# Softmaxes as separate steps, and every compute queue held to the order of the text, in a kernel of a Fourier transform and a soft mixture of experts

## The chip, the cores and the metric

The kernel runs on one core of a Trainium2 chip. The metric is the device time of one execution in microseconds. A core has five engines that run their own queues of instructions in order: TensorE (PE in the profile, with its weight loads as PEld), VectorE (DVE), ScalarE (ACT), GpSimd (POOL), and SyncE (SP), which here issues all transfers (DMA). Matmuls write to PSUM, in eight banks; VectorE and ScalarE copy results from there to SBUF ("evict" them), from where transfers take them to memory.

## The reference

The input x has 8 sequences of 2496 rows of 256 numbers, in fp32. A two-dimensional Fourier transform is taken of each sequence and its real part goes through a mixture of experts in which every token reaches every slot:

```python
X = np.fft.fft(np.fft.fft(x, axis=1), axis=2).real      # then 19968 tokens of 256
logits = tokens @ phi                                   # 32 slots
d = softmax of logits over the tokens
slot_input = d.T @ tokens                               # 8 experts, 4 slots each
h = np.maximum(slot_input[e] @ w1[e], 0.0)              # 256 -> 1024
slot_out[e] = h @ w2[e]                                 # 1024 -> 256
c = softmax of logits over the slots                    # per token
out = c @ slot_out
```

The sums in both softmaxes get 1e-9 added before the division. The output, 19968 rows of 256, is 20.4 MB.

## The kernel before, in words

The sequences are worked in four pairs, p = 0 to 3. Each pair goes through parts named by letters: a (loads are folded and projected on the slots), t, b and c (the transform's steps on the projected data, which end in the logits lt[p], their exponentials and maxima), e, d and u (the transform back, and the sum of tokens for each slot). The part m joins the four pairs' sums, l does the experts' first layer (hidden tiles h, hs, hT), v the second (so), and r spreads the experts' result over the partitions as rh, the experts' sum.

What follows concerns the output's weights c. Part s of a pair turns its logits by TensorE transposes (three PSUM banks cT, copied by ScalarE to a tile c of 128 partitions, 40 rows and 32 slots), and does the softmax over the slots in two pieces of 16 and 24 rows: VectorE takes the maximum (L531), GpSimd subtracts it (L532), ScalarE takes the exponential (L533), VectorE sums, adds 1e-9 and takes the reciprocal (L534 to L536), GpSimd multiplies (L537). Part q transposes a piece on VectorE into ct (L542). Part o makes one block of output, (p, b) with b = 0 to 4: four matmul tiles po, one for each row group g of 32 partitions of TensorE (tile_position (32 g, 0), L562), each in a PSUM bank of its own taken in turn from seven, copied by ScalarE and VectorE alternately into an output tile o (L566), and one transfer of the whole block (L570; block (0,0) goes in four). In blocks 0 to 3 a tile is one matmul of 512 columns, in block 4 two of 256 or 192. In the profile every fp32 matmul counts as two instructions. The output tiles share a ring of six with the loads of x and w1.

The text calls the parts in the order of the table ORDER. It is not the order of the queues: a scheduler takes the instructions of all parts, with the text's order as their priority, and places them engine by engine by its own estimate of when each is ready. Only SP's output transfers stand in the text's order, block after block. The parts s and q are held behind the last matmul of u by `after`. What is issued by the parts up to v keeps this freedom in both kernels.

Of the kernel before, what the change touches and what calls it, by code (L numbers as in the profile page):

```python
# [6 lines left out]
F32 = mybir.dt.float32  # L7
F32R = mybir.dt.float32r
AF = mybir.ActivationFunctionType
ALU = mybir.AluOpType  # L10
AX = mybir.AxisListType
# [3 lines left out]
NA, NCF, NKC = 64, 39, 20  # L15
NPAIR = 4
D = 256
NSLOT = 32
GS = 3
NG = 11  # L20
# [3 lines left out]
CAFTER = 1  # L24
# [4 lines left out]
CT = ['sa', 'lt', 'lt', 'lt']  # L29
HT = ['se', 'zs']  # L30
KP = ((0, 16), (16, 24))
# [14 lines left out]
).split()  # L46


# [68 lines left out]
def _build(nc, tc, xh, phih, w1h, w2h, cins, where, out):  # L117
    from contextlib import ExitStack, nullcontext

    v, sc, pe = nc.vector, nc.scalar, nc.tensor  # L120
    ctx = ExitStack()
    with ctx:
        cp = ctx.enter_context(tc.tile_pool(name="cp", bufs=1))
        sb = ctx.enter_context(tc.tile_pool(name="sb", bufs=1))
# [16 lines left out]
        def bufs_(tag):  # L141
            return {"zs": 2, "sa": 2, "se": SEB, "lt": LT}[tag]

        def bank(name, dt=F32):
            return pp.tile([128, 512], dt, name=name, tag="ps")
# [4 lines left out]
        def bank1(name, dt=F32):  # L150
            return p1.tile([128, 512], dt, name=name, tag="p1")
# [25 lines left out]
        def C(name):  # L177
            i, o, r, w = where[name]
            return cs[i][:r, o : o + w]

        ident = C("ident")
# [3 lines left out]
        ps = bank("psphi")  # L185
# [234 lines left out]
        anchor = {}  # L420
# [44 lines left out]
        def part_l(eh):  # L465
            for fh in range(2):
                ps = bank(f"h{eh}{fh}")
                for lc in range(2):
                    for g in range(4):
                        ins = pe.matmul(  # L470
                            ps[32 * g : 32 * g + 32, :], sT[:, lc, :], w1t[eh, fh, lc, g],
                            start=lc == 0, stop=lc == 1, tile_position=(0, 32 * g),
                        )
                        anchor.setdefault("l", ins.ins)
                hs = sb.tile([128, 512], F32, name=f"hs{eh}{fh}", tag="dpm", bufs=2)
                mask = sm[:, 16 + eh : 17 + eh]
                if HA:
                    sc.activation(hs, ps, AF.Relu, scale=mask)
                else:
                    v.tensor_scalar(hs, ps, 0.0, mask, op0=ALU.max, op1=ALU.mult)  # L480
                hT[eh, fh] = et([128, 16, NSLOT], f"hT{eh}{fh}")
                v.transpose(hT[eh, fh].rearrange("p f s -> p (f s)"), hs)

        def part_v(eh):
            if eh == 0:
                sos_.append(pu.tile([128, 512], F32, name="so", tag="u"))
            so = sos_[0]
            for f in range(8):
                for g in range(4):
                    ins = pe.matmul(  # L490
                        so[32 * g : 32 * g + 32, 0:D], hT[eh, f // 4][:, 4 * (f % 4) + g, :],
                        w2t[eh, f][:, g, :],
                        start=eh == 0 and f == 0, stop=eh == 1 and f == 7, tile_position=(0, 32 * g),
                    )

            anchor[f"v{eh}"] = ins.ins

        def part_r():
            so = sos_[0]
            rh.append(sb.tile([128, D], F32, name="rh", tag="mex2", bufs=1))  # L500
            sos = sb.tile([128, D], F32, name="sos", tag="dpm", bufs=2)
            ps = bank("sorep")
            sc.copy(sos[:, :128], so[:, :128])
            v.tensor_copy(sos[:, 128:], so[:, 128:D])
            for k in range(2):
                dk = slice(128 * k, 128 * k + 128)
                pe.matmul(ps[:, dk], C("sel2"), sos[:, dk], start=True, stop=True)
            v.tensor_copy(rh[0], ps[:, :D])

        hl, cq = {}, {}  # L510

        def part_s(p):
            L = lt[p]
            cq[p] = sb.tile([128, 40, NSLOT], F32, name=f"c{p}", tag=CT[p], bufs=bufs_(CT[p]))
            for b in range(3):
                ps = bank1(f"cT{p}_{b}")
                n = min(4, NG - 4 * b)
                for j in range(n):
                    pe.transpose(  # L519
                        ps[:, 120 * j : 120 * j + 120],  # L520
                        L[:, 4 * b + j].rearrange("p s k -> p (s k)"), ident[:120, :120],
                    )
                w = min(GS * n, NSLOT - 12 * b)
                sc.copy(  # L524
                    cq[p][:, :, 12 * b : 12 * b + w].rearrange("p (k h) s -> p k h s", h=2),
                    ps[:, : 40 * w].rearrange("p (s h k) -> p k h s", h=2, k=NKC),
                )
            for i, (r0, n) in enumerate(KP):
                c = cq[p][:, r0 : r0 + n]
                m = sb.tile([128, 2, 24], F32, name=f"cm{p}_{i}", tag="cm", bufs=2)[:, :, :n]  # L530
                v.tensor_reduce(m[:, 0], c, axis=AX.X, op=ALU.max)  # L531
                nc.gpsimd.tensor_tensor(c, c, m[:, 0].unsqueeze(2).to_broadcast([128, n, NSLOT]), op=ALU.subtract)  # L532
                sc.activation(c, c, AF.Exp)  # L533
                v.tensor_reduce(m[:, 1], c, axis=AX.X, op=ALU.add)  # L534
                v.tensor_scalar(m[:, 1], m[:, 1], 1e-9, None, op0=ALU.add)
                v.reciprocal(m[:, 1], m[:, 1])  # L536
                nc.gpsimd.tensor_tensor(c, c, m[:, 1].unsqueeze(2).to_broadcast([128, n, NSLOT]), op=ALU.mult)  # L537

        def part_q(p, i):
            r0, n = KP[i]  # L540
# [30 lines left out]
                    done = o  # L571

        def after(f, *a):
            at_ = {0: None, 1: anchor.get("u"), 2: anchor.get("l")}[CAFTER]
            if at_ is None:
                return f(*a)
            with tc.issue_after(at_):
                return f(*a)

        parts = {  # L580
            "a": part_a, "t": lambda p, _: part_t(p), "b": lambda p, _: part_b(p), "c": part_c,
            "e": part_e, "d": part_d, "u": lambda p, _: part_u(p), "w": lambda *_: load_w(),
            "m": lambda *_: part_m(), "l": lambda i, _: part_l(i), "v": lambda i, _: part_v(i),
            "r": lambda *_: part_r(), "s": lambda p, _: after(part_s, p), "q": lambda p, i: after(part_q, p, i), "o": part_o,
        }
        for what in ORDER:
            parts[what[0]](int(what[1]), int(what[2]))


# [54 lines left out]
```

## Time and profile before

| | |
|---|---|
| median of 3 runs | 203.22 us (203.19 to 204.41) |
| profiled execution | 203.3 us |
| its span | 201.5 us |
| mean granted TensorE clock | 0.896 |
| TensorE, VectorE, ScalarE, GpSimd busy | 172.6, 129.0, 110.7, 20.8 us |
| transfers | 59.16 MB, of which 20.45 MB written |

Times in the profile are microseconds from the span's start unless marked ns. A group's row gives line, engine, operation, output and input tiles (without their numbers), shape and count, then the busy time, the mean ns of one, the idle time of the engine just before them and what ended it. A row of a stretch gives, for PE, PEld, DVE, ACT and POOL, the busy time and in brackets the number of instructions that began there; then the granted clock (1.00 is full), the mean busy share of the 16 DMA engines and GB/s. A piece of the chain of waits gives start, duration and what ran; the chain is followed back from the last instruction. A busy PE is modelled, and is not PE at its peak.

### The profile page before, as it was taken

The numbers are of one execution on the slowest core, as the hardware profiler recorded it, in microseconds if no ns is written. First come the engines' busy times: TensorE is split into PE (matmuls) and PEld (weight loads), VectorE is DVE, ScalarE is ACT, GpSimd is POOL, SyncE is SP. The second block draws the span as 40 slices with busy tenths as digits, with TensorE's granted clock in tenths as the row PEclk, the third lists the DMA queues.
The fourth block names the chain that finished last, engine by engine and source line by source line (L and its number), as shares of the span: only waits on it lengthen the run. The fifth ranks groups of instructions, "written<-read, shape, count | busy, mean of one in ns | idle before, by whom it ended". The sixth has DMA issues, their size and how long they took to land.

```text
span 201.5 us, 4131 instructions
## 1 busy us (share of the span) xinstructions
PE 172.6 (86%) x1644; PEld 114.0 (57%) x1644; DVE 129.0 (64%) x236; ACT 110.7 (55%) x247; POOL 20.8 (10%) x25
## 2 busy tenths in 40 slices
PE   0499999899999999899999899998996999989200
PEld 0475676476678786568658593455554465756100
DVE  0599859999959936522577247977878714868300
ACT  2125775679665967677569737414947205627200
POOL 0000000000000000000000007451015204400000
PEclk9999999999999999999999999999996555557955
DMA  5999999999941998003925879911994995849994
GB/s 180 410 429 411 418 414 428 415 420 369 342 192 34 358 411 339 6 0 95 314 115 181 338 220 367 411 60 54 408 412 170 415 416 211 351 197 416 423 419 175
DMA packets 10530, 59.16 MB, mean 294 GB/s; under 512 B 1296, under 2 KB 1680, under 8 KB 5520
## 3 DMA queue, kind: packets, MB, share of 16 engines
q1 hardware_dynamic: 10512, 58.91, 74.1%
q8 instruction: 13, 0.21, 0.4%
q14 instruction: 5, 0.04, 0.1%
HBM read 38.46 MB, written 20.45 MB: 292 GB/s over the span
## 4 chain that ended last, share of the span: by engine, by line
PE 73%; ACT 7%; DVE 6%; issue 3%; DMA 2%; POOL 1%; POOLq 1%; DVEq 0%; SPq 0%; ACTq 0%
PE po L562 15%; PE pt L231 9%; PE z L238 8%; PE e L329 6%; PE a L273 5%; PE u L371 5%; PE d L346 4%; PE h L470 4%; PE so L490 3%; PE cT L519 3%; PE lp L291 3%; PE lm L292 3%; DMA x<-xh 2%; DVE o L566 2%; ACT et L232 2%
## 5 line engine op out<-in xcount | busy, mean ns | idle before, releaser
L562 PE MATMUL po<-ct,rh 32*128 32x512 f32 (+2 forms) x192 | 43.8, 700 | 2.9 <-DVE o L566 2.4
L562 PEld LDWEIGHTS po<-ct,rh 32*128 32x128 f32 x192 | 25.6, 239 | 17.7 <-DVE o L566 7.5
L231 PE MATMUL pt<-cs,eo 128*128 128x128 f32 x160 | 26.3, 295 | 8.9 <-DVE eo L226 7.8
L232 ACT COPY et<-pt 128x512 f32<-128x512 f32 x40 | 23.1, 594 | 13.8 <-PE pt L231 13.3
L566 ACT COPY o<-po 128x512 f32<-128x512 f32 (+1 forms) x40 | 21.3, 580 | 15.8 <-PE po L562 15.7
L566 DVE COPY o<-po 128x512 f32<-128x512 f32 (+1 forms) x40 | 24.6, 662 | 7.2 <-PE po L562 7.2
L231 PEld LDWEIGHTS pt<-cs,eo 128*128 128x128 f32 x160 | 19.3, 149 | 15.9 <-DVE eo L226 7.8
L224 DVE TENSOR_TENSOR x<-x 128x1024 f32<-128x1024 f32 x16 | 19.4, 1213 | 2.8 <-DMA x<-xh 2.8
L238 PE MATMUL z<-et,wphi 128*32 128x256 f32 (+1 forms) x288 | 19.0, 371 | 0.8 <-ACT et L232 0.8
L532 POOL TENSOR_TENSOR c<-c,cm 128x512 f32<-128x512 f32 (+1 forms) x8 | 10.0, 1264 | 75.3 <-DVE cm L531 72.2
L314 ACT ACTIVATE d<-lt,nm 120x128 f32<-120x128 f32 x44 | 13.6, 392 | 2.1 <-DVE nm L311 2.0
L226 DVE TENSOR_TENSOR eo<-x 128x512 f32<-128x512 f32 x20 | 13.6, 681 | 0.6 <-PE u L371 0.3
L227 DVE TENSOR_TENSOR eo<-x 128x512 f32<-128x512 f32 x20 | 13.6, 678 | 0.0
L329 PE MATMUL e<-cs,dpm 120*64 120x120 f32 x176 | 13.5, 273 | 0.0
L329 PEld LDWEIGHTS e<-cs,dpm 120*64 120x64 f32 x176 | 10.7, 136 | 3.5 <-issue 2.0
L238 PEld LDWEIGHTS z<-et,wphi 128*32 128x32 f32 x288 | 7.8, 113 | 8.3 <-ACT et L232 3.2
L354 ACT COPY ds<-d 64x320 f32<-64x320 f32 x24 | 10.0, 420 | 4.1 <-PE d L346 3.4
L273 PE MATMUL a<-cs,zt 128*120 128x128 f32 x88 | 11.4, 280 | 0.6 <-ACT zt L264 0.6
L371 PE MATMUL u<-eo,ds 128*32 128x129 f32 x320 | 11.6, 275 | 0.0
L524 ACT COPY c<-cT 128x480 f32<-128x480 f32 (+1 forms) x12 | 6.0, 516 | 10.3 <-PE cT L519 10.3
L273 PEld LDWEIGHTS a<-cs,zt 128*120 128x120 f32 x88 | 10.2, 183 | 1.9 <-ACT zt L264 1.3
L537 POOL TENSOR_TENSOR c<-c,cm 128x512 f32<-128x512 f32 (+1 forms) x8 | 10.1, 1263 | 8.4 <-DVE cm L536 8.4
(91 smaller groups left out, 213.5 us busy)
## 6 DMA issues: line engine op xcount, KB each, us to landing
x<-xh SPq DMA_DIRECT2D x16, 1024.0 KB, 11.4
out<-o SPq DMA_DIRECT2D x15, 1024.0 KB, 6.6
w<-w1h SPq DMA_DIRECT2D x6, 1024.0 KB, 9.0
w<-w2h SPq DMA_DIRECT2D x12, 512.0 KB, 6.3
x<-xh SPq DMA_DIRECT2D x4, 896.0 KB, 10.6
out<-o SPq DMA_DIRECT2D x4, 896.0 KB, 9.2
w<-w1h SPq DMA_DIRECT2D x4, 512.0 KB, 5.7
w<-w2h SPq DMA_DIRECT2D x2, 1024.0 KB, 8.3
```

The source lines that it names most:

```text
L224: v.tensor_tensor(x[:, 0:4], x[:, 0:4], x[:, 4:8], op=ALU.add)
L226: v.tensor_tensor(e[:, :, 0:128], x[:, 0:4, 0:128], x[:, 0:4, 128:256], op=ALU.add)
L227: v.tensor_tensor(e[:, :, 128:256], x[:, 0:4, 0:128], x[:, 0:4, 128:256], op=ALU.subtract)
L231: pe.transpose(b[:, g * 128 : g * 128 + 128], e[:, g, k * 128 : k * 128 + 128], ident)
L232: sc.copy(tr[k][:, :, :, qi, :], b.rearrange("p (g h a) -> p g h a", g=4, h=2))
L238: pe.matmul(z[32 * g : 32 * g + 32, o : o + n], wphi[:, w, :], tr[k][:, g].rearrange("p h q a -> p (h q a)"), start=i != 1, stop=i != 0, t ...
L273: pe.matmul(ps[:120, i * 128 : i * 128 + 128], zt[p][:, GS * g : GS * g + GS].rearrange("p s h c -> p (s h c)"), C("wa"), start=True, stop ...
L314: sc.activation(d[:, g], L[:, g], AF.Exp, bias=nm[:, g : g + 1], scale=1.0)
L329: pe.matmul(ps[64 * k : 64 * k + 64, 120 * i : 120 * i + 120], dpm[p, hf][:, k, 3 * j + i, :], C(name), start=True, stop=True, tile_positi ...
L371: last = pe.matmul(ub[32 * g : 32 * g + 32, 0:129], dsb[p][:, k, c, :], e[:, 0:129] if k == 0 else e[:, 127:256], start=cc == 0, stop=cc == 9,
L562: pe.matmul(po[:, j * w : j * w + w], rh[0][rows, 128 * dc : 128 * dc + 128], mv, start=True, stop=True, tile_position=(32 * g, 0),)
L566: (v.tensor_copy if n_ev[0] % 2 else sc.copy)(ot[:, o : o + w * len(dcs)], po[:, : w * len(dcs)])
```

## The change

The table ORDER is rewritten from the experts on. Part s becomes four steps: s (one of three groups of transposes and its copy), x (maximum and subtraction of one piece), y (its exponential), z (sum, reciprocal and multiplication). They are called one by one: the softmaxes of pairs 0 and 1 among the experts' layers, those of pairs 2 and 3 between the blocks of output of the pairs before. The parts' arithmetic is the same.

From part r on, each instruction of TensorE, VectorE, ScalarE and GpSimd gets an edge to the one that the text issued before it on the same engine. The edge orders the queue when the program is built and adds no wait on the chip. The output's transfers on SP stand as before.

```diff
@@ -40,9 +40,9 @@
...
-    "u30 m00 l00 s00 l10 q00 s10 v00 q01 v10 r00 o00 o01 q10 o02 q11 o03 "
...
+    "o00 s20 o01 s21 q11 o02 s22 o03 x20 x21 o04 y20 o10 y21 z20 o11 z21 s30 o12 q20 s31 o13 s32 x30 o14 q21 x31 "
...
@@ -509,32 +509,44 @@
 
         hl, cq = {}, {}
 
-        def part_s(p):
+        cm = {}
+
+        def part_s(p, b):
             L = lt[p]
-            cq[p] = sb.tile([128, 40, NSLOT], F32, name=f"c{p}", tag=CT[p], bufs=bufs_(CT[p]))
-            for b in range(3):
-                ps = bank1(f"cT{p}_{b}")
-                n = min(4, NG - 4 * b)
-                for j in range(n):
-                    pe.transpose(
-                        ps[:, 120 * j : 120 * j + 120],
-                        L[:, 4 * b + j].rearrange("p s k -> p (s k)"), ident[:120, :120],
-                    )
-                w = min(GS * n, NSLOT - 12 * b)
-                sc.copy(
-                    cq[p][:, :, 12 * b : 12 * b + w].rearrange("p (k h) s -> p k h s", h=2),
-                    ps[:, : 40 * w].rearrange("p (s h k) -> p k h s", h=2, k=NKC),
+            if b == 0:
+                cq[p] = sb.tile([128, 40, NSLOT], F32, name=f"c{p}", tag=CT[p], bufs=bufs_(CT[p]))
+            ps = bank1(f"cT{p}_{b}")
+            n = min(4, NG - 4 * b)
+            for j in range(n):
+                pe.transpose(
+                    ps[:, 120 * j : 120 * j + 120],
+                    L[:, 4 * b + j].rearrange("p s k -> p (s k)"), ident[:120, :120],
                 )
-            for i, (r0, n) in enumerate(KP):
-                c = cq[p][:, r0 : r0 + n]
-                m = sb.tile([128, 2, 24], F32, name=f"cm{p}_{i}", tag="cm", bufs=2)[:, :, :n]
-                v.tensor_reduce(m[:, 0], c, axis=AX.X, op=ALU.max)
-                nc.gpsimd.tensor_tensor(c, c, m[:, 0].unsqueeze(2).to_broadcast([128, n, NSLOT]), op=ALU.subtract)
-                sc.activation(c, c, AF.Exp)
-                v.tensor_reduce(m[:, 1], c, axis=AX.X, op=ALU.add)
-                v.tensor_scalar(m[:, 1], m[:, 1], 1e-9, None, op0=ALU.add)
-                v.reciprocal(m[:, 1], m[:, 1])
-                nc.gpsimd.tensor_tensor(c, c, m[:, 1].unsqueeze(2).to_broadcast([128, n, NSLOT]), op=ALU.mult)
+            w = min(GS * n, NSLOT - 12 * b)
+            sc.copy(
+                cq[p][:, :, 12 * b : 12 * b + w].rearrange("p (k h) s -> p k h s", h=2),
+                ps[:, : 40 * w].rearrange("p (s h k) -> p k h s", h=2, k=NKC),
+            )
+
+        def part_x(p, i):
+            r0, n = KP[i]
+            c = cq[p][:, r0 : r0 + n]
+            cm[p, i] = m = sb.tile([128, 2, 24], F32, name=f"cm{p}_{i}", tag="cm", bufs=2)[:, :, :n]
+            v.tensor_reduce(m[:, 0], c, axis=AX.X, op=ALU.max)
+            nc.gpsimd.tensor_tensor(c, c, m[:, 0].unsqueeze(2).to_broadcast([128, n, NSLOT]), op=ALU.subtract)
+
+        def part_y(p, i):
+            r0, n = KP[i]
+            c = cq[p][:, r0 : r0 + n]
+            sc.activation(c, c, AF.Exp)
+
+        def part_z(p, i):
+            r0, n = KP[i]
+            c, m = cq[p][:, r0 : r0 + n], cm[p, i]
+            v.tensor_reduce(m[:, 1], c, axis=AX.X, op=ALU.add)
+            v.tensor_scalar(m[:, 1], m[:, 1], 1e-9, None, op0=ALU.add)
+            v.reciprocal(m[:, 1], m[:, 1])
+            nc.gpsimd.tensor_tensor(c, c, m[:, 1].unsqueeze(2).to_broadcast([128, n, NSLOT]), op=ALU.mult)
 
         def part_q(p, i):
             r0, n = KP[i]
@@ -571,20 +583,39 @@
                     done = o
 
         def after(f, *a):
-            at_ = {0: None, 1: anchor.get("u"), 2: anchor.get("l")}[CAFTER]
-            if at_ is None:
+            if "u" not in anchor:
                 return f(*a)
-            with tc.issue_after(at_):
+            with tc.issue_after(anchor["u"]):
                 return f(*a)
+
+        traced = nc.cur_bb.bb.instructions
+        queued = {}
+
+        def in_order(f, *a):
+            n = len(traced)
+            f(*a)
+            for ins in traced[n:]:
+                if ins.engine not in (mybir.EngineType.PE, mybir.EngineType.DVE, mybir.EngineType.Activation, mybir.EngineType.Pool):
+                    continue
+                if ins.engine in queued:
+                    tc.add_manual_dep(
+                        ins, queued[ins.engine].name,
+                        mybir.DependencyInfo(mybir.DependencyClass.NoSync, mybir.DependencyReason.DATA),
+                        reason="order",
+                    )
+                queued[ins.engine] = ins
 
         parts = {
             "a": part_a, "t": lambda p, _: part_t(p), "b": lambda p, _: part_b(p), "c": part_c,
             "e": part_e, "d": part_d, "u": lambda p, _: part_u(p), "w": lambda *_: load_w(),
             "m": lambda *_: part_m(), "l": lambda i, _: part_l(i), "v": lambda i, _: part_v(i),
-            "r": lambda *_: part_r(), "s": lambda p, _: after(part_s, p), "q": lambda p, i: after(part_q, p, i), "o": part_o,
+            "r": lambda *_: part_r(), "s": lambda p, i: after(part_s, p, i), "x": lambda p, i: after(part_x, p, i), "y": lambda p, i: after(part_y, p, i),
+            "z": lambda p, i: after(part_z, p, i), "q": lambda p, i: after(part_q, p, i), "o": part_o,
         }
         for what in ORDER:
-            parts[what[0]](int(what[1]), int(what[2]))
+            f = parts[what[0]]
+            queued_ = what[0] == "r" or queued
+            in_order(f, int(what[1]), int(what[2])) if queued_ else f(int(what[1]), int(what[2]))
 
 
 def kernel(x, moe_phi, moe_w1, moe_w2):
```

How the queues stand now is read from the built programs. A name such as po1_3_2 is pair 1, block 3, row group 2 (o has pair and block, ct and cm pair and piece, cT pair and bank); the last number only tells tiles apart.

VectorE while pairs 0 and 1 are put out; before:

```order
L566 COPY o1_0_1794<-po1_0_1_1798 128x512
L566 COPY o1_1_1808<-po1_1_1_1812 128x512
L566 COPY o1_1_1808<-po1_1_3_1818 128x512
L566 COPY o1_2_1824<-po1_2_1_1828 128x512
L531 TENSOR_REDUCE cm2_0_1778<-c2_1760 128x16
L531 TENSOR_REDUCE cm2_1_1786<-c2_1760 128x24
L566 COPY o1_2_1824<-po1_2_3_1834 128x512
L534 TENSOR_REDUCE cm2_0_1778<-c2_1760 128x16
L535 TENSOR_SCALAR cm2_0_1778<-cm2_0_1778 128x16
L536 RECIPROCAL cm2_0_1778<-cm2_0_1778 128x16
L534 TENSOR_REDUCE cm2_1_1786<-c2_1760 128x24
L566 COPY o1_0_1794<-po1_0_3_1804 128x512
```

and with the change:

```order
L535 TENSOR_REDUCE cm2_0_1760<-c2_1698 128x16
L535 TENSOR_REDUCE cm2_1_1763<-c2_1698 128x24
L578 COPY o0_4_1766<-po0_4_1_1771 128x512
L578 COPY o0_4_1766<-po0_4_3_1779 128x384
L578 COPY o1_0_1785<-po1_0_1_1789 128x512
L578 COPY o1_0_1785<-po1_0_3_1795 128x512
L546 TENSOR_REDUCE cm2_0_1760<-c2_1698 128x16
L547 TENSOR_SCALAR cm2_0_1760<-cm2_0_1760 128x16
L548 RECIPROCAL cm2_0_1760<-cm2_0_1760 128x16
L578 COPY o1_1_1804<-po1_1_1_1808 128x512
L578 COPY o1_1_1804<-po1_1_3_1814 128x512
L546 TENSOR_REDUCE cm2_1_1763<-c2_1698 128x24
```

The last copy of block (1,0) moves from behind copies of blocks (1,1) and (1,2) and five softmax instructions of pair 2 to right behind the block's first; the maxima of pair 2 move ahead of the last block of pair 0.

TensorE where pair 2's output begins; before:

```order
L562 MATMUL po2_0_3_1916<-ct2_0_1822,rh_1671 128x512
L562 MATMUL po1_3_1_1842<-ct1_1_1726,rh_1671 128x512
L562 MATMUL po2_1_1_1924<-ct2_0_1822,rh_1671 128x512
L562 MATMUL po2_1_2_1927<-ct2_0_1822,rh_1671 128x512
L562 MATMUL po1_4_1_1859<-ct1_1_1726,rh_1671 128x256 x2
L562 MATMUL po2_2_0_1937<-ct2_1_1852,rh_1671 128x512
L562 MATMUL po2_2_1_1940<-ct2_1_1852,rh_1671 128x512
L562 MATMUL po2_2_2_1943<-ct2_1_1852,rh_1671 128x512
L519 MATMUL cT3_0_1873<-cs0_70,lt3_1198 128x120 x4
L519 MATMUL cT3_1_1879<-cs0_70,lt3_1198 128x120 x4
L519 MATMUL cT3_2_1885<-cs0_70,lt3_1198 128x120 x3
L562 MATMUL po2_0_0_1907<-ct2_0_1822,rh_1671 128x512
```

and with the change:

```order
L521 MATMUL cT3_2_1865<-cs0_70,lt3_1198 128x120 x3
L574 MATMUL po1_4_0_1874<-ct1_1_1725,rh_1673 128x256 x2
L574 MATMUL po1_4_1_1878<-ct1_1_1725,rh_1673 128x256 x2
L574 MATMUL po1_4_2_1882<-ct1_1_1725,rh_1673 128x192 x2
L574 MATMUL po1_4_3_1886<-ct1_1_1725,rh_1673 128x192 x2
L574 MATMUL po2_0_0_1897<-ct2_0_1843,rh_1673 128x512
L574 MATMUL po2_0_1_1900<-ct2_0_1843,rh_1673 128x512
L574 MATMUL po2_0_2_1903<-ct2_0_1843,rh_1673 128x512
L574 MATMUL po2_0_3_1906<-ct2_0_1843,rh_1673 128x512
```

The tiles of a block stand together and their row groups go 0, 1, 2, 3; the transposes of pair 3 stand a group at a time between blocks of pair 1, ahead of block (2,0).

VectorE in the experts' layers; before:

```order
L542 STREAM_TRANSPOSE ct0_1_1637<-c0_1508 128x768
L536 RECIPROCAL cm1_0_1588<-cm1_0_1588 128x16
L482 STREAM_TRANSPOSE hT11_1566<-hs11_1564 128x512
L534 TENSOR_REDUCE cm1_1_1596<-c1_1570 128x24
L542 STREAM_TRANSPOSE ct1_0_1710<-c1_1570 128x512
```

and with the change:

```order
L548 RECIPROCAL cm1_0_1586<-cm1_0_1586 128x16
L535 TENSOR_REDUCE cm1_1_1589<-c1_1568 128x24
L554 STREAM_TRANSPOSE ct0_1_1637<-c0_1508 128x768
L554 STREAM_TRANSPOSE ct1_0_1639<-c1_1568 128x512
L482 STREAM_TRANSPOSE hT11_1566<-hs11_1564 128x512
```

The transpose of pair 1's first piece, behind the hidden layer's last transpose before, stands ahead of it now.

4 rows, old and new, of the table ORDER are left out of this document.

## The prediction

> **What bounds the kernel now.** I read the page first: the span, the strip of slices, the chain's shares.
>
> ```profile
> span 201.5 us, 4131 instructions
> PE 172.6 (86%) x1644; PEld 114.0 (57%) x1644; DVE 129.0 (64%) x236; ACT 110.7 (55%) x247; POOL 20.8 (10%) x25
> ...
> PEclk9999999999999999999999999999996555557955
> DMA  5999999999941998003925879911994995849994
> HBM read 38.46 MB, written 20.45 MB: 292 GB/s over the span
> ...
> PE 73%; ACT 7%; DVE 6%; issue 3%; DMA 2%; POOL 1%; POOLq 1%; DVEq 0%; SPq 0%; ACTq 0%
> ```
>
> By shares this is a PE kernel. But the change touches nothing ahead of the softmaxes, near 118 us of 201.5, so only the last stage counts. There the strip shows holes in the DMA row while the granted clock is at half. So I asked for the busy time of the stretches between the transfers' starts and stops:
>
> ```profile
> core 0: us, PE busy (x) PEld busy (x) DVE busy (x) ACT busy (x) POOL busy (x), PEclk, DMA share, GB/s
> ...
> 140.20:152.40 12.20, 12.01 (x80) 6.91 (x76) 9.75 (x16) 8.73 (x17) 2.22 (x2) 1.00 1.01 406
> 152.40:156.00 3.60, 2.00 (x7) 1.30 (x7) 3.03 (x8) 2.67 (x5) 1.31 (x2) 0.58 0.12 48
> 156.00:168.40 12.40, 12.40 (x37) 7.00 (x36) 5.23 (x10) 2.71 (x5) 1.48 (x1) 0.50 1.00 412
> 168.40:174.00 5.60, 5.60 (x20) 3.69 (x21) 4.52 (x10) 4.38 (x8) 3.53 (x3) 0.50 0.45 187
> 174.00:176.70 2.70, 2.70 (x15) 1.57 (x8) 1.55 (x5) 1.07 (x2) 1.48 (x1) 0.50 0.94 388
> 176.70:179.10 2.40, 1.80 (x7) 0.83 (x5) 2.40 (x4) 0.58 (x1) 0.00 (x0) 0.50 0.00 0
> 179.10:198.60 19.50, 8.62 (x49) 6.05 (x47) 6.90 (x12) 5.16 (x10) 0.00 (x0) 0.68 1.01 415
> 198.60:201.50 2.90, 0.00 (x0) 0.00 (x0) 0.00 (x0) 0.00 (x0) 0.00 (x0) 0.50 0.04 15
> ```
>
> The last-but-one number is the DMA share. From 140.2 us to 198.6 the 16 DMA engines are either full (412 GB/s) or nearly idle, and for the last 10 us nothing but the output moves. The stage is bounded by the transfer of 20.45 MB and its holes are what can be won: 3.60 x 0.88 = 3.2, 5.60 x 0.55 = 3.1, 2.70 x 0.06 = 0.2 and 2.40, together 8.8 us.
>
> Next, why the queue runs dry. The DMA queue's own waits and the chain of waits from 137 us on:
>
> ```profile
> SPq L570 <- DVE o L566: 29.0, 15, 8.4
> ...
> 137.70 7.25 PE po L562 x46
> ...
> 149.51 0.60 DVE cm L531
> ...
> 150.18 2.49 POOL c L532 x2
> ...
> 154.52 0.61 DVE o L566
> ...
> 155.17 9.58 PE po L562 x20
> 164.75 2.50 PE cT L519 x11
> ```
>
> (Behind a queue's wait stand the sum in us, the number of waits and the longest.) SP issues the 20 blocks in the order of the text and stands 8.4 us for one VectorE copy. The order of before (the section on the change) names it: the last copy of block (1,0) stands on VectorE behind most of row pair 2's softmax, so at 154.52 us the block is finally complete, while later blocks that were evicted before it wait behind it on SP. The third place is alike: a tile of block (2,0) stands on TensorE behind all transposes of row pair 3 (164.75 us, 2.50 us), and the DMA falls to 0.45 at 168.4.
>
> **The change part by part.** *The queues of o, L566.* With the text's order every block is complete before the next one's copies start, so SP's head is always the oldest finished block. That removes the cause of the 8.8 us, unless a softmax step in the queue now holds the copies behind it. VectorE has the most to do:
>
> ```profile
> L566 DVE COPY o<-po 128x512 f32<-128x512 f32 (+1 forms) x40 | 24.6, 662 | 7.2 <-PE po L562 7.2
> L537 POOL TENSOR_TENSOR c<-c,cm 128x512 f32<-128x512 f32 (+1 forms) x4 | 5.0, 1262 | 5.6 <-DVE cm L536 5.6
> L532 POOL TENSOR_TENSOR c<-c,cm 128x512 f32<-128x512 f32 (+1 forms) x4 | 5.0, 1262 | 24.0 <-DVE cm L531 24.0
> L542 DVE STREAM_TRANSPOSE ct<-c 128x768 f32<-128x768 f32 (+1 forms) x5 | 4.3, 865 | 2.2 <-POOL c L537 2.2
> L534 DVE TENSOR_REDUCE cm<-c 128x16 f32<-128x512 f32 (+1 forms) x4 | 3.3, 815 | 1.9 <-ACT c L533 1.9
> L531 DVE TENSOR_REDUCE cm<-c 128x16 f32<-128x512 f32 (+1 forms) x4 | 3.1, 812 | 4.0 <-ACT c L524 4.0
> L533 ACT ACTIVATE c<-c 128x512 f32<-128x512 f32 (+1 forms) x4 | 3.0, 743 | 2.4 <-POOL c L532 2.4
> L536 DVE RECIPROCAL cm<-cm 128x16 f32<-128x16 f32 (+1 forms) x4 | 1.1, 277 | 0.1
> ```
>
> These rows cover 137.5 to 189 us. The tight point is block (2,0), the eleventh. In the new order VectorE does before its end 22 of 40 copies (22/40 x 24.6 = 13.5), three of five transposes (2.6), all four maxima (3.1), and the sums and reciprocals of pair 2 (half of 3.3 and of 1.1: 2.2; the two small additions of 1e-9 I put at half a reciprocal each, an estimate, 0.3). That is 21.7 us from the first copy:
>
> ```profile
> 131.96 0.65 DVE L482 STREAM_TRANSPOSE hT<-hs 128x512 f32<-128x512 f32 x1
> 133.41 0.95 DVE L534 TENSOR_REDUCE cm<-c 128x24 f32<-128x768 f32 x1 [0.80 <-ACT c L533]
> 134.28 0.70 DVE L542 STREAM_TRANSPOSE ct<-c 128x512 f32<-128x512 f32 x1
> ...
> 138.90 0.69 DVE L566 COPY o<-po 128x512 f32<-128x512 f32 x1 [0.37 <-PE po L562]
> ```
>
> 138.9 + 21.7 = 160.6 us. The DMA engines need block (2,0) when two pairs, 10.2 MB at 412 GB/s or 24.8 us, have gone: 140.2 + 24.8 = 165.0. So the lead is 4.4 us, and waits of VectorE up to that cost nothing. After it the lead grows: the next five blocks take ten copies (6.2) and pair 3's sums and transposes (about 4.2), 10.4 us against 12.4 of transfer. The new waits stand in that order with work ahead of them. Between the maxima and the first sum of pair 2 lie four copies, 2.5 us; the POOL subtraction and the exponential that the sum waits for take 1.26 + 0.74 = 2.0. Between that sum and its half's transpose lie the other half's sum and the copies of two blocks, 3.5 us against the 1.26 of the POOL multiplication. Should that cover fail once, a step is late by at most the 2.0.
>
> *Opening.* The first transposes of pair 2 now stand on TensorE between blocks (0,0) and (0,1), four of the eleven that took 2.50 us at half clock: 0.9, or 0.45 at full clock. ScalarE's copy of them is hidden by its idle time. When they delay block (0,1) the queue is still empty, so it counts: bounds 0 and 0.9 (half clock), I take 0.5.
>
> *The experts' stage.* On VectorE the last transpose of the hidden layer (131.96 us) now stands behind one more instruction, the transpose of pair 1 (0.70, row at 134.28): 132.7 to 133.3 us. TensorE reads it after 96 of these 128:
>
> ```profile
> 128.89 7.09 PE L490 MATMUL so<-w,hT 128*32 128x256 f32 x128
> ```
>
> 128.89 + 0.75 x 6.7 = 133.9. Covered by 0.6 us: price 0, at the worst 0.7. The transpose of pair 1's second half moves behind block (0,1); it took VectorE's idle time before, and costs about 1 us of the lead above, already counted there. POOL's new place for one subtraction before the second multiplication has the same cover.
>
> *The clock.* In the stretch 140.2 to 152.4 us TensorE did 80 matmuls in 12.2 us, 6.6 per us, at clock 1.00; in 152.4 to 156 it did 7 in 3.6 and fell to half. Paced by the transfers it will do 48 outputs and 11 transposes per 12.4 us, 4.8 per us, then 3.9 when the transposes end: between the two. So I expect half clock from about the middle of the stage. What it costs then shows a stretch at half clock in which the row groups of before happen to alternate:
>
> ```profile
> 178.30:183.20 4.90, 4.90 (x22) 4.07 (x25) 2.86 (x5) 1.55 (x3) 0.00 (x0) 0.50 0.84 341
> ```
>
> 4.90 / 22 = 0.22 us each, so 48 take 10.7 us, against 12.4 of transfer. While transposes still stand between them (2.50) a pair takes 13.2, 0.8 too long. One pair with transposes falls into the half clock: bounds 0 and 1.6 (both pairs), I take 0.8.
>
> [...]
>
> Sum: the profiled execution took 203.3 us, its span 201.5 and 1.8 around it, against a median of 203.22. 203.3 - 8.8 + 0.5 + 0.8 = 195.8.
>
> **The rivals.** *A: half clock from the first blocks on.* Then TensorE is the bound of pairs 0 and 1: 13.2 us each at the alternating rate. Without alternation a matmul takes 9.58 / 20 = 0.48 (the stretch from 155.17); three groups of transposes in each pair break the alternation, and if each break costs 0.48 a pair takes 14.6. Block (2,0) is then on its way at 137.7 + 26.4 or 29.3, plus its own eight matmuls (1.8), a copy (0.7) and 0.7 from SP's issue to the first data:
>
> ```profile
> 139.47 50.47 SPq L570 DMA_DIRECT2D out<-o  x23
> ```
>
> That is 167.3 to 170.2 against 165.0, a hole of 2.3 to 5.2, in place of the 0.8: 195.0 + 2.3 = 197.3 to 200.2, say 198.8. For it: the expected pace lies below the 6.6 per us that held the clock. Against: before, the clock stayed at 1.00 past 152.4, over the transposes of pair 2 and with waits among them. [...]
>
> *B, slower: VectorE stands still at every softmax step.* Everything behind a step waits too, copies and so TensorE's banks and SP. Per later pair the two subtractions, exponentials and multiplications that it would sit out are 4 x 1.26 + 2 x 0.74 = 6.5 us, and the wait for the transposed logits another 4.0 (row L531). Two pairs: 21.0. It decides once it exceeds lead and gain, 4.4 + 8.8 = 13.2; at the full price it gives 203.3 - 8.8 + 21.0 - 4.4 = 211, at three quarters 206. Against it speak the copies that stand between the steps.
>
> *C: the holes move.* If the softmaxes, not the scramble, set the holes, blocks (2,0) and (3,0) are late as before. The three holes sum to 8.8; with only the last, 2.4, gone but 1.1 paid it would be 202. Against: the first hole began with finished blocks waiting on SP.
>
> **How the numbers follow.** Forecast 0.68 (its own range 194 to 197), A 0.19, C 0.07, B 0.06. Under 203.3 - 8.8 = 194.5 the time falls only if the end is shorter than the 2.9 us after the last full stretch. The range 193.8 to 200.5 leaves out B, C and little else. One per cent, about what a measurement of this kernel can tell from no change, is 201.2 and 205.2: faster 0.87, same 0.07, slower 0.06.
>
> **What would show it.** In the new profile the DMA share stays near 1.0 from 140 to 189 us, SP's longest wait for a VectorE copy falls from 8.4 to under 3, and the last full stretch ends near 191. L566 keeps its 24.6 us. A shows as clock 0.5 before 145 with ScalarE and VectorE waiting for po; B as long idle times of VectorE before L546 or the transposes, ended by ACT c and POOL c; C as holes near the same blocks. I am wrong if the share is full and the time is not under 197: then the transfers themselves became slower.

## The result, and the profile after

The changed kernel takes 194.16 us (median of 4 runs, 193.23 to 194.69), the kernel before, run beside it, 203.53 (203.19 to 204.41). The ratio is 0.953, with a 95% interval of 0.948 to 0.958. The profiled execution took 194.48 us with a span of 192.6. Two of the ten runs of experiment 2 below were in a slower state, at about 210 us, and are left out of its time.

The page of the changed kernel, the lines that answer to those shown of before:

```profile
span 192.6 us, 4133 instructions
...
PE 159.6 (83%) x1644; PEld 105.1 (55%) x1644; DVE 129.4 (67%) x236; ACT 110.0 (57%) x247; POOL 20.9 (11%) x25
...
PEclk9999999999999999999999999999999999859755
DMA  5999999999991499500491596992089999999994
...
PE 63%; DVE 13%; DMA 8%; ACT 6%; issue 3%; DVEq 0%; SPq 0%; ACTq 0%
```

```profile
L578 DVE COPY o<-po 128x512 f32<-128x512 f32 (+1 forms) x40 | 24.9, 662 | 5.4 <-PE po L574 4.1
```

VectorE, ScalarE and GpSimd have the busy time they had, and VectorE's copies take 24.9 us for 24.6; the DMA row has no hole left behind the experts' stage. The stretches of the output stage, from the same view as before (busy time of PE, PEld, DVE, ACT and POOL with the number of instructions that ran in the stretch, those that cross a border counted on both sides of it; then clock, DMA share, GB/s):

```profile
133.80:140.20 6.40, 5.50 (x62) 2.89 (x56) 3.31 (x7) 1.63 (x4) 1.48 (x1) 1.00 0.00 0
140.20:144.00 3.80, 3.33 (x26) 1.44 (x22) 2.88 (x5) 3.11 (x7) 0.00 (x0) 1.00 0.94 364
144.00:152.40 8.40, 7.70 (x52) 4.30 (x52) 7.67 (x15) 6.17 (x13) 3.54 (x3) 1.00 1.01 413
152.40:156.00 3.60, 3.56 (x21) 1.85 (x19) 3.53 (x8) 2.80 (x6) 1.48 (x1) 1.00 1.02 423
156.00:168.40 12.40, 8.73 (x64) 4.72 (x68) 12.23 (x23) 7.28 (x14) 5.05 (x4) 0.96 1.01 419
168.40:174.00 5.60, 5.60 (x27) 3.47 (x28) 4.55 (x8) 2.48 (x5) 0.00 (x0) 0.50 1.01 414
...
179.10:189.00 9.90, 0.00 (x0) 0.00 (x0) 0.00 (x0) 0.00 (x0) 0.00 (x0) 0.60 1.01 419
189.00:192.60 3.60, 0.00 (x0) 0.00 (x0) 0.00 (x0) 0.00 (x0) 0.00 (x0) 0.50 0.21 86
```

The transfers start where they did, at about 140.2 us, and run full to 189.0 instead of 198.6. VectorE is now busy 12.23 of 12.40 us in the middle stretch and TensorE 8.73. SP's longest wait for a VectorE copy (the last number) falls from 8.4 to 2.5 us:

```profile
SPq L582 <- DVE o L578: 31.0, 20, 2.5
```

What set the holes before can be read when each copy of the two traces is matched to its row in the built queue. For each block, the end of its third and of its last copy, which row group's tile was last, and when SP issued the transfer:

```
before  block  third   last    g  issue  |  changed  third   last    g  issue
        (1,0)  145.57  155.12  3  155.18 |           149.75  150.12  3  150.18
        (1,1)  148.91  154.98  2  155.61 |           151.85  152.45  3  152.51
        (1,2)  151.56  157.86  2  157.89 |           154.40  154.99  3  155.06
        (1,3)  156.68  161.00  1  161.03 |           156.19  156.78  3  156.85
        (1,4)  159.21  163.78  1  163.80 |           158.10  158.56  3  158.62
        (2,0)  160.41  169.89  0  169.91 |           160.88  161.47  3  161.54
```

SP issued a block within 0.1 us of its last copy, with one exception of 0.6. It did not sit on finished blocks: there were none. Every one of these six blocks of before had three tiles copied and lacked the fourth, for 4 to 10 us. The number of the missing tile is not random. Counted through the output, the po tiles take seven PSUM banks in turn (bank, bank3, bank1, bank3, bank, bank1, bank3), and the missing tile of each of these six blocks is the one that falls on bank1, the two banks that the next pair's transposes cT also use. The last hole, from 176.7 us, is alike: SP issued block (2,2) at 178.28 us, behind a VectorE copy that ended at 178.21, and in TensorE's queue of before (the section on the change) tiles 0, 1 and 2 of this block stand ahead of pair 3's transposes without tile 3, the one on bank1. That became the first theory to test.

### The profile page after: what moved, and what is told of

The parts are those of the page before. It is cut to its first block, busy times and chain, and to the rows that moved or that the text cites. A ratio compares the mean times of both kernels' runs of the same rounds, so it can differ in the third digit from the quotient of the medians.

```text
span 192.6 us, 4133 instructions
## 1 busy us (share of the span) xinstructions
PE 159.6 (83%) x1644; PEld 105.1 (55%) x1644; DVE 129.4 (67%) x236; ACT 110.0 (57%) x247; POOL 20.9 (11%) x25
## 4 chain that ended last, share of the span: by engine, by line
PE 63%; DVE 13%; DMA 8%; ACT 6%; issue 3%; DVEq 0%; SPq 0%; ACTq 0%
PE pt L231 10%; PE z L238 8%; DVE o L578 7%; PE e L329 7%; PE a L273 6%; PE u L371 6%; DMA out<-o 5%; PE d L346 4%; PE h L470 4%; PE so L490 4%; PE lp L291 3%; PE lm L292 3%; PE po L574 3%; DMA x<-xh 2%; ACT et L232 2%
## 5 line engine op out<-in xcount | busy, mean ns | idle before, releaser
L574 PE MATMUL po<-ct,rh 32*128 32x512 f32 (+2 forms) x192 | 31.6, 608 | 5.4 <-DVE o L578 2.6
L578 DVE COPY o<-po 128x512 f32<-128x512 f32 (+1 forms) x40 | 24.9, 662 | 5.4 <-PE po L574 4.1
L574 PEld LDWEIGHTS po<-ct,rh 32*128 32x128 f32 x192 | 17.2, 203 | 15.7 <-DVE o L578 8.2
L273 PE MATMUL a<-cs,zt 128*120 128x128 f32 x88 | 11.4, 279 | 0.6 <-ACT zt L264 0.6
L354 DVE COPY ds<-d 64x320 f32<-64x320 f32 x8 | 3.9, 484 | 10.2 <-PE d L346 10.1
```

The costliest lines, as they stand in the source:

```text
L273: pe.matmul(ps[:120, i * 128 : i * 128 + 128], zt[p][:, GS * g : GS * g + GS].rearrange("p s h c -> p (s h c)"), C("wa"), start=True, stop ...
L354: (v.tensor_copy if DE >> (2 * h + k) & 1 else sc.copy)(dst, src)
L574: pe.matmul(po[:, j * w : j * w + w], rh[0][rows, 128 * dc : 128 * dc + 128], mv, start=True, stop=True, tile_position=(32 * g, 0),)
L578: (v.tensor_copy if n_ev[0] % 2 else sc.copy)(ot[:, o : o + w * len(dcs)], po[:, : w * len(dcs)])
```

## The experiments

Eleven kernels were run, each beside the kernel before on the same chip. The ratios are to the kernel before, which took 202.54 to 203.53 us at these times, so a cost beside the changed kernel can differ by up to 1 us between times and ratios; "lag" is the longest time between the third and the last copy of a block of pairs 0 to 2.

| edit | us | ratio, 95% | longest wait of SP for a VectorE copy | lag |
|---|---|---|---|---|
| changed kernel | 194.16 | 0.953 (0.948 to 0.958) | 2.5 | 0.6 |
| 1 own banks, nothing held | 203.85 | 1.004 (1.002 to 1.006) | 6.8 | 2.2 |
| 2 steps and new order, nothing held | 203.42 | 1.002 (0.999 to 1.005) | 7.1 | 10.4 |
| 3 whole softmaxes, all held | 205.93 | 1.013 (1.009 to 1.018) | 11.4 | 0.6 |
| 4 row groups in pairs, all held | 195.37 | 0.962 (0.959 to 0.965) | 2.0 | 0.9 |
| 5 changed, own banks | 193.35 | 0.953 (0.951 to 0.956) | 2.5 | 1.0 |
| 6 changed, 3 more VectorE steps | 193.81 | 0.955 (0.953 to 0.957) | 5.6 | 0.6 |
| 7 changed, 8 more VectorE steps | 199.22 | 0.982 (0.979 to 0.986) | 10.6 | 0.6 |
| 8 own banks, later softmaxes, nothing held | 204.60 | 1.008 (1.006 to 1.011) | 7.0 | 2.8 |
| 9 TensorE alone held | 200.20 | 0.987 (0.984 to 0.990) | 6.4 | 2.2 |
| 10 VectorE and ScalarE alone held | 200.20 | 0.987 (0.982 to 0.992) | 4.4 | 1.3 |
| 11 as 10, with own banks | 194.91 | 0.960 (0.955 to 0.965) | 2.5 | 1.0 |

(6 and 7 are one edit in two sizes.)

### 1. Banks of their own

```diff
-        BANKS = [bank, bank3, bank1, bank3, bank, bank1, bank3]
+        BANKS = [bank, bank3, bank3, bank, bank3]
...
-                po = BANKS[n_ev[0] % 7](f"po{p}_{b}_{g}")
+                po = BANKS[n_ev[0] % 5](f"po{p}_{b}_{g}")
```

> The kernel before, with one edit: the output tiles po take five PSUM banks in turn instead of seven, and the two banks of p1 are left to the softmaxes' transposes cT alone. Nothing is held to the text's order. Theory 'banks': in the kernel before a tile of each block is left behind because it shares two banks with the transposes of the next pair; with banks of its own the blocks finish in order, the DMA share stays near 1.0 from about 142 us on, and the time is 194 to 198 us. Rival 'VectorE': the left-behind tile is late because its copy stands behind softmax steps on VectorE, which this edit does not hold; holes of 5 us or more remain and the time is 200 to 204.

Measured: 203.85 us, in the range of the rival 'VectorE'. The theory was right about the tile and wrong about the time. No tile of pairs 1 and 2 is left behind any more: the last copy of their blocks follows the third by at most 0.7 us. But the transposes, with two banks that nothing else asks for, are now done by the scheduler in the experts' stage already, and the softmaxes of pairs 2 and 3 stand on VectorE in front of the first blocks. The chain of waits of this kernel at its output's start:

```profile
137.57 0.47 PE cT L519 x3
...
138.53 1.55 DVE cm L531 x2
140.07 0.34 DVE rh L508
...
142.54 0.69 DVE o L566
143.23 0.86 DVE cm L534
144.09 0.59 DVE cm L531
...
147.35 0.95 DVE cm L531
...
148.59 0.64 DVE o L566
```

rh comes 2.9 us later than before (140.07 against 137.22), and VectorE goes from the first copy to softmax steps. Block (0,1) is issued at 152.9 us, 11.4 later than before, and from 153.8 on the transfers run full (418 GB/s). The holes went from the middle to the front, and there softmax steps on VectorE stand in the chain, as the rival has it for the middle. So shared banks explain which tile was late, and are not all that has to be put right.

### 2. The steps without the holding

```diff
-            queued_ = what[0] == "r" or queued
-            in_order(f, int(what[1]), int(what[2])) if queued_ else f(int(what[1]), int(what[2]))
+            f(int(what[1]), int(what[2]))
```

> The changed kernel without the holding: softmaxes as separate steps in the new order of the text, but no edges between the instructions of an engine. Theory 'banks': the scheduler again gives the shared banks to transposes first and leaves tiles behind; holes of 4 to 9 us, 198 to 204 us. Rival 'steps': splitting the softmaxes and calling them earlier is what helps, and the holding adds nothing: 194 to 196 us.

Measured: 203.42 us. As the banks' theory has it, tiles are left behind again, by up to 10.4 us, in block (1,4), and again they are those on the shared banks. The hole that ends with this block follows a stretch at full clock, so a hole does not need the half clock of before:

```profile
157.00:166.80 9.80, 8.47 (x49) 4.57 (x49) 5.45 (x9) 4.73 (x10) 2.02 (x2) 1.00 0.94 388
166.80:171.60 4.80, 0.86 (x3) 0.51 (x6) 3.31 (x8) 1.80 (x3) 2.83 (x3) 0.72 0.01 6
```

Splitting the softmaxes and calling them earlier gives nothing by itself: the order of the text is a priority there and no more.

### 3. Whole softmaxes, everything held

```diff
         for what in ORDER:
-            parts[what[0]](int(what[1]), int(what[2]))
+            f = parts[what[0]]
+            queued_ = what[0] == "r" or queued
+            in_order(f, int(what[1]), int(what[2])) if queued_ else f(int(what[1]), int(what[2]))
```

(with `in_order` as in the change; table and parts as before)

> The kernel before, with its own order of the text and whole softmaxes, but every compute queue held to that order from the experts' sum on. This is rival B of the prediction made real: VectorE stands still through the whole softmax of pair 2 behind block (0,4) and of pair 3 behind block (1,4). A softmax took 149.4 to 158.8 us before, 9.4 us. Worked out: VectorE reaches the end of block (0,4) near 146, stands until 155.4, and block (1,0) leaves at 157.4 against 152.6, a hole of 4.8; the same again for pair 3, 4.9: 194.2 + 9.7 = 204 us, 201 to 207. Rival 'holding alone': the order of blocks is all that matters and the steps' places do not: 194 to 197.

Measured: 205.93 us, 1.3% slower than before and inside the range of 201 to 207. The stretches of this kernel's output:

```profile
154.40:159.00 4.60, 3.03 (x8) 1.74 (x12) 3.46 (x7) 2.78 (x5) 1.64 (x2) 0.50 0.00 0
159.00:171.40 12.40, 7.78 (x55) 4.95 (x49) 8.02 (x14) 5.29 (x10) 2.33 (x3) 0.85 1.00 412
171.40:177.00 5.60, 3.00 (x8) 1.71 (x12) 3.43 (x7) 2.77 (x5) 2.67 (x2) 0.64 0.00 0
```

Two holes, 4.6 and 5.6 us, for 4.8 and 4.9 worked out, one for each softmax that stands whole in the queue. Every block is complete and in order here, so order of blocks alone is worth nothing if a softmax is in line without copies between its steps.

### 4. Row groups that follow themselves

In part o, blocks 0 and 1, and 2 and 3, are done together:

```diff
+            bs = [b] if b == 4 else [b, b + 1]
...
             for g in range(4):
+                for x in bs:
```

> The changed kernel with the output's blocks 0 and 1, and 2 and 3, done together, row group by row group: TensorE's order is group 0 of both, group 1 of both and so on, so that a matmul follows one on its own row group half the time. All queues stay held. Theory 'row groups': the alternation is what makes the stage fast, above all at half clock; TensorE needs twice as long for a pair of blocks and the time goes to 199 or more. Rival 'order alone': TensorE has slack beside the transfers, the time is 194 to 196.5, with at most 1 to 2 us for the first transfer, which waits for two blocks' copies to alternate.

Measured: 195.37 us, 1.2 us over the changed kernel by times, 1.8 by ratios, in the range of 'order alone'. In blocks 0 to 3 every second tile now follows one on its own row group, and the transfers are still nearly full:

```profile
144.00:168.40 24.40, 21.49 (x130) 12.63 (x126) 23.05 (x40) 17.30 (x33) 8.58 (x7) 0.93 0.98 403
168.40:189.00 20.60, 10.78 (x48) 7.82 (x48) 9.15 (x17) 5.46 (x10) 1.48 (x1) 0.61 1.01 417
```

The alternation is not what brings the gain; half of it is worth at most 1 to 2 us, in which the pairs of blocks, which finish together, have their part too.

### 5. The changed kernel with banks of its own

The edit of experiment 1 in the changed kernel.

> The changed kernel with the five-bank rule of the first experiment: po tiles never share banks with the transposes. Theory 'banks': the holding already settles who gets a bank, so nothing is left to win: 193.5 to 195. If the five banks are too few to keep TensorE ahead, up to 197.

Measured: 193.35 us, 0.15 under the theory's range; the ratio to before is that of the changed kernel within both intervals. Once the queues are held, who shares banks with whom no longer matters.

### 6 and 7. The lead of VectorE

```diff
-            v.transpose(t.rearrange("p k s -> p (k s)"), ...)
+            for _ in range(4 if (p, i) == (2, 1) else 1):      # 9 in the second kernel
+                v.transpose(t.rearrange("p k s -> p (k s)"), ...)
```

> The changed kernel with three more VectorE transposes of 128x768 (0.97 us each, 2.9 us; the same result is written again) just before pair 2's second piece is done, ahead of block (2,0). Theory 'transfers bound, VectorE leads': block (2,0) is issued at 161.5 us in the changed kernel and the transfers reach it at about 165, a lead of 3.5 us, so it costs 0 to 0.5 us: 194 to 195. Rival 'VectorE is the bound': it costs all of it, 197.

> As the run with three, with eight more transposes, 7.8 us of VectorE. Theory 'transfers bound, VectorE leads by 3.5': a hole of 7.8 - 3.5 = 4.3 us just before block (2,0) and none after it, 198 to 199. Rival 'VectorE is the bound': 202. Rival 'the lead grows by the ring': nothing, 194.

Measured: 193.81 and 199.22 us. Three more transposes (2.9 us) cost nothing that can be measured, eight (7.8 us) cost 5.1 beside the changed kernel's 194.16, and 5.4 beside the kernel with three. In the second kernel the hole stands where it was expected, just before block (2,0) is issued at 168.8 us:

```profile
156.00:165.80 9.80, 2.87 (x23) 1.12 (x17) 9.49 (x12) 2.94 (x6) 1.05 (x1) 0.78 0.86 359
165.80:169.60 3.80, 1.43 (x6) 1.24 (x10) 3.80 (x6) 0.49 (x1) 1.48 (x1) 0.50 0.00 0
169.60:172.00 2.40, 2.40 (x17) 1.64 (x13) 2.33 (x6) 1.61 (x4) 0.86 (x1) 0.57 1.06 437
```

3.80 us empty and 9.80 x 0.14 = 1.4 before it, 5.2 in all: 7.8 of work against a lead of 2.6 to 2.9. So the transfers bound the stage, and the lead is a little less than the 3.5 expected, which counts up to SP's issue: with the 0.7 us from issue to the first data, which the prediction reads from the first block, it is 2.8.

### 8. Own banks, and the softmaxes later

Experiment 1, and the transposes of pair 2 placed behind block (0,1) on TensorE, those of pair 3 behind block (1,1):

```diff
+            at_ = anchor.get({2: (0, 1), 3: (1, 1)}.get(a[0]), at_) if f is part_s else at_
             with tc.issue_after(at_):
```

> The first experiment (kernel before, output tiles in five banks of their own, no holding) with one more edge: the transposes of pair 2 are held on TensorE behind block (0,1), those of pair 3 behind block (1,1). In the first experiment the blocks finished whole but the softmaxes of pairs 2 and 3 all came in front of the first blocks. Theory 'two causes': a tile left behind in shared banks, or a softmax in front of a block that the transfers wait for, each makes the holes; with both gone and still nothing held on VectorE or ScalarE the time is 194 to 198 us. Rival 'VectorE must be held': the softmaxes that the scheduler packs together on VectorE still cost 5 us or more, 199 to 204.

Measured: 204.60 us; the theory fell, its rival held (0.6 us above its range). No tile is left behind in a bank and no softmax stands at the front, but the scheduler packs each softmax on VectorE around one block. Its copies wait with it:

```profile
140.20:149.80 9.60, 7.87 (x48) 4.54 (x44) 6.39 (x11) 6.26 (x13) 3.36 (x3) 0.97 0.82 329
149.80:155.00 5.20, 4.15 (x12) 1.95 (x12) 4.51 (x10) 1.34 (x4) 1.65 (x2) 0.50 0.65 268
155.00:161.00 6.00, 6.00 (x22) 3.10 (x22) 2.00 (x4) 2.29 (x5) 0.00 (x0) 0.50 1.00 411
161.00:171.00 10.00, 8.88 (x35) 5.05 (x30) 7.37 (x14) 4.89 (x9) 3.58 (x4) 0.50 0.34 139
```

Here the clock is at half from 149.8 to 171 us, and the transposes of pair 3 fall into it; at a DMA share of 0.34 over 10 us the second softmax costs 6.6 us, about twice the first, which costs 3.5 in the first two rows (9.60 x 0.18 and 5.20 x 0.35, the opening among them). How much of that is the clock and how much the packed softmax this run does not separate.

### 9 to 11. Which queue has to be held

The change holds four engines; here TensorE alone, then VectorE and ScalarE alone, then these two again with banks of their own:

```diff
-                if ins.engine not in (mybir.EngineType.PE, mybir.EngineType.DVE, mybir.EngineType.Activation, mybir.EngineType.Pool):
+                if ins.engine not in (mybir.EngineType.PE,):                                          # 9
+                if ins.engine not in (mybir.EngineType.DVE, mybir.EngineType.Activation):             # 10, 11
```

> The changed kernel with only TensorE held to the order of the text; VectorE, ScalarE and GpSimd are free. The queues that the build makes then have every block's tiles together on TensorE, and on VectorE the softmax of pair 2 packed around block (0,3). Theory 'TensorE's order decides' (it settles which tile gets a shared bank): 194 to 197 us. Rival 'VectorE must be held': 199 to 204.

> The changed kernel with only VectorE and ScalarE held; TensorE and GpSimd are free. TensorE then mixes tiles of two blocks, and copies wait in line for tiles that TensorE does late. Theory 'TensorE's order decides': copies stand still behind late tiles, but no tile falls far behind, since its copy cannot be passed: 195 to 200 us. Rival 'the copies' order is all': 194 to 195.5, as with everything held.

> VectorE and ScalarE held, TensorE and GpSimd free, as in the experiment before it, which took 200.2 us; but the output tiles have five banks of their own and the transposes' two banks to themselves. The built queue then has the blocks whole on TensorE without any hold there. Theory 'banks, then VectorE': holding TensorE was needed only because tiles and transposes share banks; without the sharing the copies' order is enough, 193.5 to 195.5 us. Rival 'TensorE must be held for its own sake' (its transposes come earlier and stand in front of outputs): 198 to 201.

Measured: 200.20, 200.20 and 194.91 us. In 9 the rival came true, in 10 the theory's mechanism at 0.2 us above its range, in 11 the theory. Either hold alone brings about a quarter of the gain (1.3% of 4.7%). With TensorE held the tiles come in order, but VectorE packs its softmaxes; with VectorE and ScalarE held the copies stand in line for tiles that TensorE does late (stretches of 9, then of 10):

```profile
149.90:151.70 1.80, 1.60 (x5) 0.76 (x8) 1.80 (x5) 0.02 (x1) 1.30 (x1) 0.50 0.01 5
...
166.60:172.00 5.40, 4.26 (x14) 2.19 (x17) 3.75 (x7) 0.67 (x2) 1.48 (x1) 0.50 0.58 241
```

```profile
161.00:165.00 4.00, 4.00 (x17) 2.93 (x18) 1.42 (x3) 1.41 (x4) 1.05 (x1) 0.50 0.65 268
165.00:170.00 5.00, 4.76 (x15) 2.52 (x17) 5.00 (x9) 3.32 (x6) 1.48 (x1) 0.50 0.55 228
```

The last of the three settles what TensorE's hold is for: with the banks separate, TensorE needs none, and the time is 0.8 us above the changed kernel's (1.5 by the ratios). What can be seen of that is the opening: eight transposes of pair 2 are now done in the experts' stage, and rh comes at 138.0 instead of 137.2.

So there were two causes, and both had to go. On TensorE, tiles and transposes shared two banks, and the scheduler's order gave the banks to the transposes. On VectorE, softmax steps stood packed in front of copies that the transfers needed next. Removing one of them moved the holes and won a quarter or nothing.

## Why the prediction was right, and where it was not

- *The bound and the size.* The forecast was 195.8 us, the time is 194.16. The 8.8 us of holes are gone. From the profiles: 8.8 won, 0.2 lost in the opening (3.80 us at 0.94), about 0.7 won because the full stretches ran at some 418 GB/s for 412, 0.7 lost in a longer end (3.6 us behind the last full stretch for 2.9, at a share of 0.21), 8.6 in all against 8.9 of span. The prediction had the time come under 194.5 only by a shorter end; it came to 194.16 with a longer one, by the faster transfers. The last full stretch ended at 189.0, not near 191.
- *The cause of the holes* is the step that failed. It said that SP held finished blocks behind an unfinished one. There were no finished blocks; each lacked one tile, the one in a shared bank. What the prediction said the change does, that blocks become complete one by one, was right all the same, and so the size came out; that is luck in part, since the change removed a cause that the prediction did not name. Its two readings of single tiles hold: the copy of (1,0) stood behind the softmax on VectorE, the tile of (2,0) behind the transposes on TensorE. But for (1,0) the softmax was the end of the delay and not its start: the third copy ended at 145.57 us and the last began at 154.44, while TensorE's last tile of 512 columns before it ended at 151.42. So at least 3.0 us of the 8.9 are VectorE's, and how the rest divides is not shown. In experiment 1, without shared banks and with VectorE free, the lag was gone; its softmaxes no longer stood among these copies either, so it does not separate the two.
- *The lead of VectorE* was put at 4.4 us at block (2,0). VectorE finished it at 161.5, 0.9 later than the 160.6 worked out, and experiments 6 and 7 give a lead between 2.6 and 2.9. The sum of busy times left out two waits of VectorE for tiles, 0.95 and 0.66 us, that ended at 141.12 and 145.12, and the lead left out the 0.7 us from issue to the first data. It was enough.
- *The opening* was put at 0.5 and cost 0.2.
- *The clock* was put at 0.8 and cost nothing. It was expected to halve in the middle of the stage, while transposes still stood between the outputs; it halved only at about 167 us, behind the last of them. The reading of the pace behind the term was wrong as well. The granted clock of 0.58 in 152.4 to 156 puts the halving of before about 0.6 us into that stretch, and TensorE's only pause of it came later, from 153.6 to 155.2, so the slow pace there cannot have brought it. The new kernel's clock fell within a pause of 2.2 us without a matmul (the last section has the rows). Without this term the sum is 195.0, near the profiled 194.48.
- *The experts' stage* was put at 0: rh came at 137.20, before at 137.22, with the last transpose of the hidden layer begun at 132.33, ahead of the 132.7 worked out.
- *Rival A* did not come, since the clock stayed full to about 167 us. Its mechanism, transposes at half clock, is there in experiment 8, but not by itself.
- *Rival B*, made real in experiment 3, cost about what its price said: 205.93 against 206 at three quarters. The three quarters were a choice, so that the two agree so closely is luck. That the copies between the steps keep it away is shown by the two kernels together.
- *Rival C*, holes that only move, is what experiments 1 and 8 are. It was given 7 in 100 for the change; with one of the two causes left it is what happens. The 1.1 us that its price adds has no working; the opening and the clock of the sum are 1.3.

## What to carry to other kernels

When a transfer stage has holes, ask of each block which tile was last and in which buffer it lay, before blaming the queue that issues it: here, in the six blocks of the table, it was every time the tile that shared its PSUM banks with other work. In this stage, bounded by transfers, the other engines had a lead that can be counted, 2.6 to 2.9 us at block (2,0), and the softmaxes' steps, called with copies between them, left no hole from 144.0 to 189.0 us; whole softmaxes in the held queue made holes of 4.6 and 5.6 us (experiment 3). Separate one cause and the holes may only move, so price what is next in line before counting the gain.

## What the runs showed of the hardware

In these profiles TensorE's busy time does not tell when the granted clock halves or returns. The changed kernel around the place where it halved:

```profile
140.20:168.40 28.20, 23.32 (x157) 12.31 (x157) 26.32 (x47) 19.35 (x38) 10.07 (x8) 0.98 1.00 410
163.00:166.00 3.00, 2.87 (x22) 1.49 (x19) 2.86 (x8) 2.13 (x5) 1.05 (x1) 1.00 1.05 432
166.00:168.00 2.00, 0.00 (x0) 0.00 (x0) 2.00 (x5) 0.48 (x2) 1.48 (x1) 0.83 0.97 405
168.00:174.00 6.00, 5.89 (x27) 3.77 (x30) 4.95 (x9) 2.48 (x5) 0.00 (x0) 0.50 1.02 416
174.00:176.00 2.00, 2.00 (x21) 1.76 (x16) 1.68 (x4) 1.36 (x4) 0.00 (x0) 0.96 1.00 414
```

and the kernel before, ahead of its halving:

```profile
149.50:152.90 3.40, 3.21 (x21) 2.00 (x17) 2.97 (x7) 1.31 (x3) 2.48 (x2) 1.00 0.94 390
```

In the changed kernel, at 157 matmuls in the 28.2 us from 140.2 to 168.4, 5.6 per us, the clock held until about 167.3. It halved within a pause of 2.2 us without a matmul, from 165.9 to 168.1, and came back about 6 us after the matmuls had begun again, at 27 in 6.0 us, 4.5 per us. Before, 37 in 12.4 us (3.0 per us, from 156.0 to 168.4) did not bring it back, though the profile calls TensorE busy for 12.40 us of them. Nor is it the count of matmuls alone: before, the clock fell at about 153 us right behind 21 in 3.4 us, 6.2 per us. TensorE paused for 0.2 us in all in these 3.4 us. What brings the fall and the return these runs do not settle.

Doing two blocks' tiles on the same row group in turn, half of the alternation taken away, changed the time by 1 to 2 us (experiment 4): beside transfers at 403 and 417 GB/s TensorE was busy 21.49 of 24.40 and 10.78 of 20.60 us, so there was slack for it.
